# Seven more small loads of x on ScalarE's queue, at the head of a one-token attention and feed-forward kernel

## The chip, the cores and the metric

The kernel runs on one core of one Trainium2 chip. The metric is the device time of one execution in microseconds (us). The kernel before takes 407.94 us, the median of three runs (407.80 to 408.14).

## What is computed

One decode step for one token: an attention block with a key and value cache, then a gated feed-forward block, each behind a layer norm and each added to its input. All tensors are bf16; D = 1024, 32 query heads share 4 key/value heads, the cache holds 65536 positions of 128 numbers, and the feed-forward width is 3584.

```python
h  = x + A(layernorm(x))         # q = x @ wq; softmax(q k^T / sqrt(128)) v; @ wo
h2 = h + B(layernorm(h))         # (gelu(x @ w_gate) * (x @ w_up)) @ w_down
```

Keys and values are 4 x 65536 x 128 numbers each, 67.1 MB apiece; the five weight matrices add 38.8 MB. Nearly all of it is read once and used for one row of x.

## The kernel before

**Staging.** A large SBUF buffer, `ring`, has three slots of 128 partitions x 64 KB. The function `load` (L179 issues the DMA) takes the slots in turn and issues every large load on SyncE's queue, in this order: `wq` (8.39 MB, one slot); then for each key/value head K in two loads and V in two loads of 8.39 MB each, K running one head ahead of V; then `wo`, `w_gate`, `w_up`, and `w_down` in five pieces. A load into a slot waits until the engines have read what the slot held. The texts call the first two K loads K1 and K2 (head 0, first and second half), the third K3 (head 1, first half).

**The head of the kernel.** VectorE clears `x_row` (L183). ScalarE's queue then loads x, 4 rows of 512 bytes, into `x_row` (L184); this is the only load on that queue. The `wq` load is issued by SyncE first of all: a step at the end of the build moves it in front of the start barrier. After L184, ScalarE runs a short exponential (L197, `warm`) that brings in its table. When x has landed, VectorE turns it (`x_t`, L231), the layer norm follows (VectorE, with two short TensorE sums and a power on GpSimd), and its result goes into `xnz` (L238). TensorE then multiplies by `wq` (`q_ps`), once `wq` has landed. The result goes through VectorE (`q_t`, L261) and TensorE into ScalarE's copies into `wsel` (L269).

**The attention loops.** For each half head the K slot is turned in place by VectorE (L288), TensorE forms the scores (`qk_ps`), ScalarE and VectorE make the softmax, and TensorE multiplies by V (`acc_ps`). Near the end of the attention VectorE copies a 32 x 128 block into `o_sb`, a small buffer that nothing touches until then.

**The tail.** The last two loads are halves of the last row block of `w_down`. Four short matmuls (`fb_ps`), one copy (`o_fin`, L601) and the store of the output (L602) follow.

**Completion counters.** Every load on SyncE's and ScalarE's queues counts its completion on one of eight semaphores, DMAHW0 to DMAHW7, which the build hands out in turn over both queues together. A load's counter reaches its mark when all of the load has landed. A load that gets a counter which an earlier load has used waits, on the engine that issues it, until that earlier load has landed. In the kernel before, the first loads have these counters: `wq` 0, x 1, K1 2, K2 3, K3 4; K1 and K2 have no wait at all.

Of the kernel before, what the change touches and what calls it, by code (L numbers as in the profile page):

```python
# [17 lines left out]
def kernel(  # L18
# [13 lines left out]
    nc = tc.nc  # L32
# [50 lines left out]
    o_sb = lead.tile([Hq, Dh], BF16, name="o_sb")  # L83
# [88 lines left out]
    def load(src, off=0):  # L172
        n, w = src.shape[1], src.shape[2]
        if off == 0:
            slot[0] = (slot[0] + 1) % NSLOT
        assert off + n * w <= 2 * CW
        o = slot[0] * 2 * CW + off
        tv = ring[:, o:o + n * w].rearrange("p (n w) -> p n w", w=w)
        loads.append(nc.sync.dma_start(out=tv, in_=src).ins)  # L179
        return tv  # L180
# [3 lines left out]
    nc.scalar.dma_start(out=x_row[0:97:32, :], in_=A_x[0, 0].rearrange("(g n) -> g n", g=4))  # L184
    assert DC * HD == 2 * CW
    wq_t = load(wq_v[:])

    make_identity(nc, ident_bf[:])
    make_identity(nc, ident_f[:])
# [11 lines left out]
    for bp in range(4):  # L201
        s0 = 64 * (bp // 2) + bp % 2
        nc.vector.tensor_copy(out=esel[:, bp, :, :],
                              in_=ident_bf[:, s0:s0 + 63:2].unsqueeze(1).to_broadcast([P, 4, 32]))
# [391 lines left out]
    for b, put in ((0, nc.vector.tensor_copy), (1, nc.scalar.copy)):  # L596
        wv = load(wd_v[:, c0:FC, b * HW:(b + 1) * HW], c0 * D + b * HW)
        down_rows(wv, c0, 1, [b])
        if b == 1:
# [3 lines left out]
                      in_=o_b[0:97:32, :, :])  # L603
# [30 lines left out]
```

## Time and profile before

| | |
|---|---|
| median of three runs | 407.94 us |
| span of the profiled execution, first to last instruction | 406.0 us |
| own time of the profiled execution | not listed apart from its span |
| median of the runs less that span | 1.94 us |
| TensorE busy | 295.5 us (73%) |
| VectorE busy | 203.8 us (50%) |
| ScalarE busy | 40.0 us (10%) |
| SyncE's DMA queue (q1) | 173.02 MB, 98.7% of the time of 16 DMA engines |
| ScalarE's DMA queue (q10) | 8 packets, 2 KB |

The span runs from the first to the last instruction of one profiled execution; the time of a run holds that and what lies around it. Busy shares are averages over the whole span. The share of a DMA queue is the time that its packets took, over the span of all 16 DMA engines. In the timeline, an engine name with a q (SPq, ACTq) is the engine's instruction that issues a DMA, not the transfer.

### The profile page before, as it was taken

The numbers are of one execution on the slowest core, as the hardware profiler recorded it, in microseconds if no ns is written. First come the engines' busy times: TensorE is split into PE (matmuls) and PEld (weight loads), VectorE is DVE, ScalarE is ACT, GpSimd is POOL, SyncE is SP. The second block draws the span as 40 slices with busy tenths as digits, with TensorE's granted clock in tenths as the row PEclk, the third lists the DMA queues.
The fourth block names the chain that finished last, engine by engine and source line by source line (L and its number), as shares of the span: only waits on it lengthen the run. The fifth ranks groups of instructions, "written<-read, shape, count | busy, mean of one in ns | idle before, by whom it ended". The sixth has DMA issues, their size and how long they took to land.

```text
span 406.0 us, 2610 instructions
## 1 busy us (share of the span) xinstructions
PE 295.5 (73%) x1519; PEld 59.4 (15%) x681; DVE 203.8 (50%) x186; ACT 40.0 (10%) x62; POOL 7.5 (2%) x17
## 2 busy tenths in 40 slices
PE   0160777758899695979969957997696999646196
PEld 0110111111111110221111113111110211211012
DVE  0210989999839744971595387609943000220210
ACT  1000000023000031100000302000021100100000
POOL 2000000000000000000000000000010000000000
PEclk9995689987899999769999967899999699886689
DMA  9999999999999999999999999999999999999995
GB/s 413 413 413 471 458 413 415 413 466 452 413 421 420 471 439 413 428 420 471 433 420 428 420 465 433 420 435 420 458 433 420 441 420 458 399 442 447 400 423 225
DMA packets 3631, 173.18 MB, mean 427 GB/s; under 512 B 416, under 2 KB 676, under 8 KB 804
## 3 DMA queue, kind: packets, MB, share of 16 engines
q1 hardware_dynamic: 3612, 173.02, 98.7%
q8 instruction: 8, 0.13, 0.1%
q14 instruction: 3, 0.02, 0.0%
q10 hardware_dynamic: 8, 0.00, 0.0%
HBM read 173.02 MB, written 0.00 MB: 426 GB/s over the span
## 4 chain that ended last, share of the span: by engine, by line
DMA 41%; PE 35%; DVE 21%; ACT 2%; issue 1%; ACTq 0%; DVEq 0%
DMA ring<-in_A_k_cache_dram 30%; DVE ring L288 16%; PE acc_ps L158 16%; DMA ring<-in_B_w_down_dram 11%; PE qk_ps L156 6%; PE qk_ps L158 5%; PE acc_ps L156 5%; DVE mx L313 2%; ACT sc L309 2%; DVE pT L346 1%; PE o_ps L156 1%; PE at_ps L156 1%; DVE acc_sb L369 1%; PE at_ps L158 1%; PE nb_ps L156 0%
## 5 line engine op out<-in xcount | busy, mean ns | idle before, releaser
L288 DVE STREAM_TRANSPOSE ring<-ring 128x2048 uint32<-128x2048 uint32 x64 | 142.6, 2279 | 36.9 <-DMA ring<-in_A_k_cache_dram 36.9
L156 PE MATMUL qk_ps<-ring,wsel 128*128 128x512 bf16 x256 | 107.4, 420 | 50.2 <-DVE ring L288 31.2
L158 PE MATMUL qk_ps<-ring,wsel 128*128 128x512 bf16 x256 | 106.6, 416 | 0.0
L158 PE MATMUL acc_ps<-ring,pT 128*128 128x512 bf16 x384 | 105.1, 383 | 0.0
L156 PEld LDWEIGHTS <-wsel 128*128 128x128 bf16 x256 | 27.1, 106 | 157.3 <-issue 140.4
L156 PE MATMUL acc_ps<-ring,pT 128*128 128x512 bf16 x128 | 49.1, 384 | 0.0
L313 DVE TENSOR_REDUCE mx<-qk_ps 128x1 f32<-128x1024 f32 x16 | 19.5, 1220 | 24.7 <-ACT sc L309 18.7
L346 DVE STREAM_TRANSPOSE pT<-pT 128x1024 bf16<-128x1024 bf16 x16 | 19.3, 1228 | 23.8 <-ACT pT L340 23.8
L309 ACT COPY sc<-qk_ps 128x1024 f32<-128x1024 f32 x12 | 12.1, 1012 | 149.5 <-PE qk_ps L158 149.5
L156 PEld LDWEIGHTS <-pT 128*128 128x128 bf16 x128 | 12.8, 100 | 90.7 <-issue 90.6
L369 DVE COPY acc_sb<-acc_ps 32x512 f32<-32x512 f32 x8 | 5.3, 667 | 29.4 <-PE acc_ps L158 29.3
L340 ACT ACTIVATE pT<-sc,nbias 128x1024 bf16<-128x1024 f32 x12 | 13.7, 1141 | 44.9 <-DVE nbias L332 41.9
L156 PE MATMUL wu_ps<-ring,hnz 128*32 128x448 bf16 x32 | 5.9, 729 | 9.0 <-DMA ring<-in_B_w_up_dram 9.0
L156 PE MATMUL ln_tot<-ln_s,ones_f 128*128 128x1 f32 x8 | 1.9, 312 | 13.5 <-DVE ln_s L210 11.7
L156 PE MATMUL q_ps<-ring,xnz 128*32 128x512 bf16 x32 | 5.0, 598 | 8.9 <-DMA ring<-in_A_wq_dram 8.9
L156 PE MATMUL wg_ps<-ring,hnz 128*32 128x448 bf16 x32 | 5.9, 718 | 7.2 <-DMA ring<-in_B_w_gate_dram 7.2
L156 PE MATMUL o_ps<-sel,acc_sb 128*128 128x8 f32 x32 | 6.6, 335 | 5.8 <-DVE rl L383 5.4
L371 ACT COPY acc_sb<-acc_ps 32x512 f32<-32x512 f32 x8 | 4.6, 578 | 58.6 <-DVE acc_sb L369 58.5
L512 DVE STREAM_TRANSPOSE wu_t<-wu_ps 128x448 f32<-128x448 f32 x2 | 1.2, 630 | 14.2 <-PE wu_ps L156 14.2
L261 DVE STREAM_TRANSPOSE q_t<-q_ps 128x512 f32<-128x512 f32 x2 | 1.3, 694 | 13.8 <-PE q_ps L158 13.8
L512 DVE STREAM_TRANSPOSE wg_t<-wg_ps 128x448 f32<-128x448 f32 x2 | 1.2, 628 | 13.4 <-PE wg_ps L156 13.4
L340 ACT ACTIVATE pT<-qk_ps,nbias 128x1024 bf16<-128x1024 f32 x4 | 4.5, 1114 | 29.8 <-PE acc_ps L158 16.8
(108 smaller groups left out, 94.2 us busy)
## 6 DMA issues: line engine op xcount, KB each, us to landing
ring<-in_B_w_gate_dram SPq DMA_DIRECT2D x1, 7168.0 KB, 35.5
ring<-in_B_w_up_dram SPq DMA_DIRECT2D x1, 7168.0 KB, 38.6
ring<-in_B_w_down_dram SPq DMA_DIRECT2D x1, 4096.0 KB, 39.6
ring<-in_B_w_down_dram SPq DMA_DIRECT2D x1, 2048.0 KB, 43.6
ring<-in_B_w_down_dram SPq DMA_DIRECT2D x1, 768.0 KB, 45.0
ring<-in_B_w_down_dram SPq DMA_DIRECT2D x2, 128.0 KB, 44.8
ring<-in_A_k_cache_dram SPq DMA_DIRECT2D x8, 38.6
ring<-in_A_v_cache_dram SPq DMA_DIRECT2D x8, 34.4
```

What stands on the lines that cost most here:

```text
L156: return pe(t.matmul(out, lhsT=lhsT, rhs=rhs, start=start, stop=stop, tile_position=tile_position, skip_group_check=skip_group_check))
L158: op = t.add_instruction(mybir.InstMatmult(name=nc.get_next_instruction_name(), engine=t.engine, start_tensor_calc=start, stop_tensor_calc ...
L261: nc.vector.transpose(out=q_t[:, k, :], in_=q_banks[k])
L288: dv(nc.vector.transpose(out=kt[:, c * w:(c + 1) * w], in_=kt[:, c * w:(c + 1) * w]))
L309: ac(nc.scalar.copy(out=sc[:], in_=flat))
L313: dv(nc.vector.tensor_reduce(out=state[("mx", g)][:, li:li + 1], in_=flat, axis=AX.X, op=ALU.max))
L340: ac(nc.scalar.activation(out=flat, in_=state.pop(("sc", g, li)), func=ACT.Exp, bias=st["nbias"][:, 0:1], scale=scale, accum_out=st["lpart ...
L346: dv(nc.vector.transpose(out=flat, in_=flat))
L369: dv(nc.vector.tensor_copy(out=acc_sb[sl, :], in_=acc[sl, c, :]))
L371: ac(nc.scalar.copy(out=acc_sb[sl, :], in_=acc[sl, c, :]))
L512: nc.vector.transpose(out=t[:, k, :], in_=banks[k][:, 0:HF * 32])
```

## The change

Seven loads are added in the source behind the `wq` load, on ScalarE's queue. Load i (0 to 6) reads the first 16n numbers of x, with n = 2i + 2, into n partitions x 16 numbers (32 bytes) of `o_sb`: 2, 4, 6, 8, 10, 12 and 14 rows, 56 rows and 1792 bytes in all. `o_sb` is written over before it is read, so nothing that is computed changes.

```diff
     nc.scalar.dma_start(out=x_row[0:97:32, :], in_=A_x[0, 0].rearrange("(g n) -> g n", g=4))
     assert DC * HD == 2 * CW
     wq_t = load(wq_v[:])
+    for i in range(7):
+        n = 2 * i + 2
+        nc.scalar.dma_start(out=o_sb[0:n, i * 16:(i + 1) * 16], in_=A_x[0, 0, 0:16 * n].rearrange("(p n) -> p n", n=16))
 
     make_identity(nc, ident_bf[:])
```

## The prediction

> **What bounds the kernel now.** I read the page first, its slices and its DMA queues.
>
> ```profile
> DMA  9999999999999999999999999999999999999995
> GB/s 413 413 413 471 458 413 415 413 466 452 413 421 420 471 439 413 428 420 471 433 420 428 420 465 433 420 435 420 458 433 420 441 420 458 399 442 447 400 423 225
> DMA packets 3631, 173.18 MB, mean 427 GB/s; under 512 B 416, under 2 KB 676, under 8 KB 804
> ...
> q1 hardware_dynamic: 3612, 173.02, 98.7%
> ```
>
> The reader is to see that the DMA engines are busy in every slice but the last; no other engine comes near (TensorE 73%). SyncE's queue q1 fills 98.7% of the span. In the trace's packet records nearly every 64 KB packet takes 2.418 us on its engine, at the start as at the end, which is 16 x 65536 B / 2.418 us = 433.6 GB/s; 173.02 MB at that rate are 399.0 us. So the kernel is one unbroken stream of loads. The rate is that of a busy engine, so time in which the engines stand idle between two loads does not come back.
>
> The chain that ended last confirms the end of it: the last load, then under 1 us of work and the store.
>
> ```profile
> 358.13 44.71 DMA ring<-in_B_w_down_dram
> 402.84 0.04 issue
> 402.88 0.27 PE fb_ps L156 x4
> 403.15 0.02 issue
> 403.17 0.27 ACT o_fin L601
> ```
>
> Further back this chain names VectorE, TensorE and ScalarE, but only because a load's issue waits for its slot. What matters is whether the issue comes before the load ahead of it has landed. The closest case in SyncE's timeline is the V load issued at 111.83 us; the load ahead of it lands at 119.90 us (packet landings in the trace), so 8.1 us early. The stream never starves there, nor would it if loads and work behind them moved together.
>
> Third, the timeline of the first 30 us, where the change sits.
>
> ```profile
> 0.00 0.38 SPq L179 DMA_DIRECT2D ring<-in_A_wq_dram  x1
> ...
> 0.78 0.81 SPq L179 DMA_DIRECT2D ring<-in_A_k_cache_dram  x2
> ...
> 1.07 1.09 ACTq L184 DMA_DIRECT2D x_row<-in_A_x_dram  x1
> ...
> 3.49 0.20 ACT L197 ACTIVATE warm<-neg_half 128x1 f32<-128x1 f32 x1
> 9.82 0.63 DVE L231 STREAM_TRANSPOSE x_t<-x_row 128x256 bf16<-128x256 bf16 x1 [8.63 <-DMA x_row<-in_A_x_dram]
> ...
> 14.62 0.10 PEld L156 LDWEIGHTS <-xnz 128*32 128x32 bf16 x1 [1.72 <-DVE xnz L238]
> 21.85 0.62 PE L156 MATMUL q_ps<-ring,xnz 128*32 128x512 bf16 x4 [8.87 <-DMA ring<-in_A_wq_dram]
> ```
>
> Two things are to be seen. K1 and K2 are issued at 0.78 us, 21 us before `wq` has landed, so each engine goes from its last `wq` packet straight into K1. And x is wanted late: its layer norm is done at 14.62 us, TensorE waits for `wq` until 21.85 us, so x has 21.85 - 14.62 = 7.2 us to spare.
>
> **What the change moves.** The built order of the two programs, with their waits, shows it. Before:
>
> ```
> SP   ring<-in_A_k_cache_dram 128x32768 x2
> SP   ring<-in_A_k_cache_dram 128x32768 [waits DMAHW0,PE]
> ACT  x_row<-in_A_x_dram 4x256 [waits DVE]
> ```
>
> After:
>
> ```
> SP   ring<-in_A_k_cache_dram 128x32768 [waits DMAHW1]
> SP   ring<-in_A_k_cache_dram 128x32768 [waits DMAHW2]
> SP   ring<-in_A_k_cache_dram 128x32768 [waits DMAHW3,PE]
> ACT  o_sb 2x16 / x_row 4x256 [waits DVE] / o_sb 4x16, 6x16, 8x16, 10x16, 12x16 / o_sb 14x16 [waits DMAHW0]
> ```
>
> The seven loads use up the eight counters. In the built order the load of 2 rows has counter 0, `wq` 1, x 2, the loads of 4 to 12 rows 3 to 7; the load of 14 rows is back at 0, K1 at 1, K2 at 2. So K1 now waits for all of `wq` to land, K2 for x, K3 for the load of 4 rows, and ScalarE's last small load for the first. That wait of K1 is the change.
>
> **The sum: the gap in front of K1.** In the packet records each engine's last `wq` packet ends between 20.99 and 21.48 us, on average 21.26. The last landing is counted at 21.81, and TensorE, which waits for the same landing, starts at 21.85. Take 21.85 us for K1's issue. How long a load takes from issue into an empty stream the trace shows once on this queue, for `wq` itself: issued at 0.00, first packets start between 1.00 and 1.75 us, and they take 2.48 to 3.48 us where later ones take 2.418; they end between 4.08 and 4.58, on average 4.35. Less one plain packet that is an effective start at 4.35 - 2.42 = 1.93 us after issue. K1 then runs effectively from 21.85 + 1.93 = 23.78 us instead of 21.26: 2.52 us lost on each engine. Bounds: if the longer first packets belong to the cold start alone, packets start on average 1.22 us behind the issue and the loss is 21.85 + 1.22 - 21.26 = 1.8 us. The store of the output, the other issue into an empty queue, has its first packet 1.28 us after its issue (403.46 to 404.74) where `wq` has 1.00, but its issue is 0.3 us longer too. At the other end, with those 0.3 us for K1 too, it is 2.8 us. I take 2.5, by `wq`'s row, which is the same queue and the same shape.
>
> **What costs nothing.** K2's wait: x has landed long before. K3 was issued at 28.41 us, when TensorE was done with `q_ps`; the small loads have been served by then, at the latest in the gap, where ScalarE's queue has the engines to itself. ScalarE's issues: seven times at most 1.09 us (x's row) are 7.6 us, plus the wait of the last for the first until about 10 us; behind them stand only the table load and `warm`, and ScalarE's next work (L269) is at 30.35 us. If that cover were gone it would still reach only `wsel`, wanted at 43.53 us. The packets: 56 rows and 56 count writes at x's rates (27 and 9 ns) are 2.0 us over 16 engines, 0.25 us on an engine that has a part of all seven; about half of it falls into the gap. I add 0.1 us. `o_sb`'s later overwriting waits for loads that landed 300 us earlier.
>
> x itself gets the load of 2 rows ahead of it. In the packet records x's rows go out at 6.65 us and its count writes at 9.08 us: one small packet per engine and 2.42 us round between q1's packets. Where an engine has both loads, x is two rounds later, 4.84 us, and has 7.2 to spare: 2.4 us remain. Even past that only `q_ps`, the K work and the slots behind them come later, and the stream has 8.1 us or more in hand.
>
> The sum is 2.5 + 0.1 = 2.6 us. Everything behind K1's landing (41.15 us) moves with the stream, up to the store; against the profiled execution the span becomes 406.0 + 2.6 = 408.6 us, and with the 1.94 us by which the median lies over that span, 410.5 us.
>
> **The rivals.** (a) The gap is shorter. Between the end of `wq`'s issue (0.38) and its first packet (1.00) lie 0.62 us; if only these pass behind the wait, on all engines at once and with plain packets, the loss is 21.85 + 0.62 - 21.26 = 1.2 us; with the issue's own 0.38 before them it is 1.6. With the 0.1 for small packets that is 409.2 to 409.6 us. For it: the store's 256-byte packets took 15 to 18 ns each, no long start. Against it: all 16 first `wq` packets are longer than 2.42 us. The Trainium skill, "DMA: Bandwidth & Descriptors" (section Specifications), gives a first-byte latency of about 0.6 us for loads issued by the sync and scalar engines; by that alone the time would be an estimated 409.2 us. The trace has that figure only behind the end of the issue.
>
> (b) The gap opens, and the time stays: 407.9 us. It needs 2.5 us of idle elsewhere to be regained; q1's own 98.7% leave 5.3 us, of which 1.0 lies before the first packet and over 1 behind the last load. Little speaks for it.
>
> (c) Faster. The engines drift apart in the stream: `wq`'s landings lie within 0.49 us, the last load's within 2.1 us (400.71 to 402.84), with a mean of 401.8. A gap sets all engines off together again; if that drift were mended whole, the end would come 1.0 us earlier. It decides from a gap under 0.2 us, as 1.0 must beat the gap by 0.8; the time would then be about 407.1 us. Against it: the drift at 21 us is small and grows afterwards.
>
> (d) The small packets cost far more than x's: 14 of them on the two engines that have a part of every small load, at 0.1 us each instead of 0.02, are 1.4 us, some of it ahead of `wq`'s last packet. Price: 411.3 to 412 us. For it: 32-byte rows are not in the trace. Against it: 4-byte writes take 9 ns there and 256-byte rows 15 to 18 ns. Of like size is the case that a small load lands so late that K3 or the next V load waits. The skill's same page (section on the increment by 16) says that such a load uses the lowest-numbered engines, one for each row here; by that the first two engines carry a packet of all seven. No run here shows it yet.
>
> **How the numbers follow.** The gap as worked out, 409.7 to 411.2 us: 0.80. (a) 0.08, (b) 0.04, (c) 0.02, (d) 0.06. A measurement of this kernel tells apart about 0.2%, 0.8 us, so (b) is the same, (c) faster, and all others are slower: 0.94. The range goes from 409.3, into (a), to 411.5, into (d).
>
> **What would show it.** In the profile after, the timeline has K1's issue at 21.8 to 22.0 us right behind `wq`'s landing instead of 0.78, with K2's behind it; the packets have none of q1's between about 21.5 and 22.8 us; the stretch of 20 to 25 us shows a DMA share near 0.6; VectorE's first L288 starts at 43.5 to 44 us instead of 41.15; q1's share falls to about 98.1%. ScalarE shows eight issues, L231 starts by 15 us and `q_ps` still at 21.9. The prediction is wrong if K1's issue comes early, if the gap is there and the end does not move, or if a second gap opens behind it.

## The result, and the profile after

| | before | after |
|---|---|---|
| median | 407.87 us (4 runs) | 410.53 us (4 runs) |
| ratio | | 1.0064 (95% interval 1.0052 to 1.0076) |
| span of the profiled execution | 406.0 us | 408.8 us (its own time: 410.55 us) |

The changed kernel is slower by 2.66 us; 410.5 us were forecast, with a range of 409.3 to 411.5.

The page of the changed kernel, slices and DMA queues:

```profile
DMA  9979999999999999999999999999999999999995
...
DMA packets 3743, 173.18 MB, mean 424 GB/s; under 512 B 528, under 2 KB 788, under 8 KB 916
...
q1 hardware_dynamic: 3612, 173.02, 98.2%
...
q10 hardware_dynamic: 120, 0.00, 0.0%
```

One digit has changed: the third slice (20.4 to 30.7 us) stands at 7. SyncE's queue q1 moved the same 3612 packets and 173.02 MB, in 98.2% of a longer span. ScalarE's queue q10 has 120 packets in place of 8, too little to show as a share.

The timeline of the head shows which wait stands there:

```profile
0.00 0.39 SPq L179 DMA_DIRECT2D ring<-in_A_wq_dram  x1
...
1.39 0.59 ACTq L184 DMA_DIRECT2D x_row<-in_A_x_dram  x1
...
2.02 7.85 ACTq L189 DMA_DIRECT2D o_sb<-in_A_x_dram  x6
9.90 1.28 ACT L200 ACT_TABLE_LOAD   x1 [9.90 <-DMA o_sb<-in_A_x_dram]
...
14.49 0.63 DVE L234 STREAM_TRANSPOSE x_t<-x_row 128x256 bf16<-128x256 bf16 x1 [13.28 <-DMA x_row<-in_A_x_dram]
...
21.95 5.50 SPq L179 DMA_DIRECT2D ring<-in_A_k_cache_dram  x3
21.98 0.62 PE L156 MATMUL q_ps<-ring,xnz 128*32 128x512 bf16 x4 [4.32 <-DMA ring<-in_A_wq_dram]
...
43.73 4.50 DVE L291 STREAM_TRANSPOSE ring<-ring 128x2048 uint32<-128x2048 uint32 x2 [15.06 <-DMA ring<-in_A_k_cache_dram]
```

SyncE issues K1 at 21.95 us in place of 0.78. TensorE's first `q_ps` matmul, which waits for the same landing of `wq`, starts 0.03 us behind that issue. VectorE's first work on K1 comes at 43.73 us, 2.58 later than before. SyncE's own waits name the releaser:

```profile
SPq L179 <- DMA ring<-in_A_wq_dram: 21.2, 1, 21.2
```

In the kernel before, a line of nearly the same figures (20.2 us, once) belonged to K3 and cost nothing, because K1 and K2 were queued already. The label alone does not tell whether a wait costs; what the DMA engines still have queued at that time does.

The stretch of the gap, by windows (the columns behind the two times: length, busy time of PE, PEld, DVE, ACT and POOL, then TensorE's clock, the DMA share and GB/s):

```profile
20.00:25.00 5.00, 3.02 (x32) 0.72 (x19) 0.00 (x0) 0.00 (x0) 0.00 (x0) 1.00 0.62 210
```

The kernel before has a share of 0.97 and 419 GB/s there, two packets an engine where this one has one; a packet counts here whole, in the stretch in which it starts. The end of the chain is as it was, later by 2.78 us:

```profile
362.94 42.68 DMA ring<-in_B_w_down_dram
405.62 0.04 issue
405.66 0.26 PE fb_ps L156 x4
405.93 0.02 issue
405.95 0.27 ACT o_fin L604
```

### The profile page after: what moved, and what is told of

Read it like the earlier page. It is cut to its first block, busy times and chain, and to the rows that moved or that the text cites. A ratio compares the mean times of both kernels' runs of the same rounds, so it can differ in the third digit from the quotient of the medians.

```text
span 408.8 us, 2621 instructions
## 1 busy us (share of the span) xinstructions
PE 296.7 (73%) x1519; PEld 58.8 (14%) x681; DVE 203.9 (50%) x186; ACT 40.0 (10%) x62; POOL 7.5 (2%) x17
## 3 DMA queue, kind: packets, MB, share of 16 engines
q1 hardware_dynamic: 3612, 173.02, 98.2%
HBM read 173.02 MB, written 0.00 MB: 423 GB/s over the span
## 4 chain that ended last, share of the span: by engine, by line
DMA 41%; PE 39%; DVE 17%; ACT 2%; issue 1%; ACTq 0%; DVEq 0%
DMA ring<-in_A_k_cache_dram 25%; PE acc_ps L158 16%; DVE ring L291 12%; DMA ring<-in_B_w_down_dram 10%; PE qk_ps L156 8%; PE qk_ps L158 7%; DMA ring<-in_A_wq_dram 5%; PE acc_ps L156 5%; DVE mx L316 2%; ACT sc L312 1%; DVE pT L349 1%; PE o_ps L156 1%; PE at_ps L156 1%; DVE acc_sb L372 1%; PE at_ps L158 1%; ACT acc_sb L374 1%
## 5 line engine op out<-in xcount | busy, mean ns | idle before, releaser
L156 PE MATMUL qk_ps<-ring,wsel 128*128 128x512 bf16 x256 | 108.4, 423 | 53.2 <-DVE ring L291 33.8
L158 PE MATMUL qk_ps<-ring,wsel 128*128 128x512 bf16 x256 | 107.8, 421 | 0.0
```

The costliest lines, as they stand in the source:

```text
L156: return pe(t.matmul(out, lhsT=lhsT, rhs=rhs, start=start, stop=stop, tile_position=tile_position, skip_group_check=skip_group_check))
L158: op = t.add_instruction(mybir.InstMatmult(name=nc.get_next_instruction_name(), engine=t.engine, start_tensor_calc=start, stop_tensor_calc ...
```

## The experiments

The theory: K1 gets the counter that `wq` holds, so it waits until `wq` has landed, and the DMA engines stand idle from `wq`'s last packet until K1's packets flow. The rivals: the small packets on the DMA engines cost the time; ScalarE's issues or the late x do; or part of the gap is regained. Each kernel was timed beside the kernel before, which stood at 407.70 us in the first group (the first four rows) and at 407.87 us in the second; the ratios are to these.

| kernel | K1 issued, us | median, us | ratio (95% interval) |
|---|---|---|---|
| six small loads | 9.49 | 407.78 | 1.0002 (0.9994 to 1.0011) |
| eight small loads | 14.27 | 407.93 | 1.0006 (0.9997 to 1.0014) |
| no small load, K1 waits for `wq` | 22.12 | 410.30 | 1.0062 (1.0050 to 1.0075) |
| no small load, K1 waits for `q_ps` | 27.20 | 416.00 | 1.0202 (1.0188 to 1.0216) |
| two breaks | 21.81; K2 43.69 | 412.92 | 1.0123 (1.0109 to 1.0137) |
| seven small loads, counters handed out otherwise | 9.64 | 407.77 | 1.0000 (0.9991 to 1.0009) |
| fifteen small loads | 23.51 | 412.15 | 1.0105 (1.0091 to 1.0118) |
| the changed kernel again | 21.93 | 410.25 | 1.0059 (1.0046 to 1.0072) |

**Six and eight small loads.**

```diff
-    for i in range(7):
+    for i in range(6):        # the other kernel: range(8)
```

> Six small loads in place of seven (the one of 14 rows is left out). In the built order K1 now has the counter of the load of 2 rows and K2 that of wq. If the wait of K1 for wq is the whole cost, K1 is issued when the load of 2 rows has landed, at about 10 us, long before wq's last packet at 21.3 us; K2 is issued at 21.95 us, with K1 still running until 41 us; no gap opens, and the time is that of the kernel before plus at most 0.1 us: 407.8 to 408.1 us. If the small packets on the DMA engines are the cost, 42 of 56 rows should leave about three quarters of the 2.66 us: about 409.9 us. If ScalarE's issues or the late x are the cost, x lands as late as with seven (14.4 us), and six of seven parts remain: about 410.1 us.

> Eight small loads in place of seven (one of 16 rows is added, 72 rows in all). K1 has x's counter, K2 that of the load of 4 rows; the eighth small load has wq's counter, and it is ScalarE that waits for wq. If the wait of K1 for wq is the whole cost, K1 is issued when x has landed, at about 14.5 us, no gap opens, and more small loads are faster than seven: 407.8 to 408.2 us. ScalarE then issues its last small load at about 22 us and brings its table in by 24.5 us, ahead of its copies into wsel at about 29 us, so that costs nothing. If the small packets or ScalarE's issues are the cost, 72 rows against 56 give about 411.3 us, slower than with seven.

SyncE's issues in the timeline of the first and of the second:

```profile
9.49 19.07 SPq L179 DMA_DIRECT2D ring<-in_A_k_cache_dram  x3
```

```profile
14.27 13.05 SPq L179 DMA_DIRECT2D ring<-in_A_k_cache_dram  x3
...
22.26 1.28 ACT L200 ACT_TABLE_LOAD   x1 [22.26 <-DMA ring<-in_A_wq_dram]
```

With six loads K1 waits for a small load, with eight for x; both issue it well before 21 us, and no gap opens: the DMA share of 20 to 25 us is 0.98 and 0.97. The time is that of the kernel before. With eight the wait for `wq` has moved to ScalarE, whose table load comes at 22.26 us and still ends ahead of its copies into `wsel` at 28.94. Six and eight loads cost nothing and seven cost 2.66 us: a cost that grows with the packets or with the issues cannot give that. x lands as late as with seven (`x_t` at 14.46 and 14.35 us), so the late x is out as well.

**The wait without the small loads.**

```diff
     t = load((k_v if what == "k" else v_v)[g][:, li * LN:(li + n) * LN, :])
+    if len(loads) in (2, 3):
+        tc.add_manual_dep(loads[-1], loads[0].name, ...)      # K1, K2 behind wq
```

> The kernel before, without any small load, but K1 and K2 wait for wq to land. If the wait is the whole cost, the gap is that of the kernel after without the small packets: K1 is issued at 21.85 us, its first packets start 0.95 to 2 us later and are longer than 2.42 us, K1 lands 2.5 us later than in the kernel before, and the time is 410.3 to 410.6 us. If the small loads matter beside the wait, the time lies between 407.9 and 410.2 us, by as much as they cost. x lands at 9.8 us as in the kernel before.

```profile
22.12 6.75 SPq L179 DMA_DIRECT2D ring<-in_A_k_cache_dram  x3
22.14 0.62 PE L156 MATMUL q_ps<-ring,xnz 128*32 128x512 bf16 x4 [9.16 <-DMA ring<-in_A_wq_dram]
```

The wait alone gives 1.0062, the changed kernel gave 1.0064, and the windows show 0.63 as the DMA share of 20 to 25 us, where the changed kernel has 0.62. The whole loss is reproduced without one small load. K1 is issued 0.27 us later than expected, with `wq`'s landing, which this run shows at 22.1 us.

**A gap three times as long.**

```diff
+    q_last = latest["pe"]                # TensorE's last q_ps matmul
...
+    if len(loads) in (2, 3):
+        tc.add_manual_dep(loads[-1], q_last.name, ...)
```

> As the kernel in which K1 waits for wq, but K1 and K2 wait for TensorE's last q_ps matmul, at 27.1 to 28.4 us, so that the gap is three times as long. If the stream regains nothing, the engines lose from 21.26 us to 1.93 us behind K1's issue, 7.8 to 9.1 us, and the time is 415.7 to 417.0 us: each microsecond of later issue is one microsecond of time. If some of a gap is hidden by work elsewhere or given back by a faster stream, the loss is smaller than that, and the gap of 2.5 us was perhaps not lost whole either.

```profile
27.20 1.28 SPq L179 DMA_DIRECT2D ring<-in_A_k_cache_dram  x3
```

K1 is issued 5.08 us later than with the wait for `wq`, and the time rises by 5.7 us, from 410.30 to 416.00; the fastest of its five runs, 415.31, is 5.0 us above. Nothing of a longer gap is regained. From the packet records, the engines lost 7.8 us up to K1's first packets (31.43 us, their mean end, less 2.42 for a plain packet, less 21.21, the mean end of `wq`); the median rose by 8.3. The profiled run of this kernel has a stretch of slightly longer packets between 65 and 155 us, 0.06 to 0.18 us each; behind 30 us its packets take 0.62 us an engine more in all than those of the kernel before. That is about the rest.

**Two breaks.**

```diff
+    if len(loads) in (2, 3):
+        tc.add_manual_dep(loads[-1], loads[-2].name, ...)     # K1 behind wq, K2 behind K1
+    if len(loads) == 4: ...                                   # K3 stays behind K2, without a wait
```

> Without small loads; K1 waits for wq to land and K2 waits for K1 to land, so the stream breaks twice. If each break costs what the first one did, from the last packet of one load to 1.9 us behind the next one's issue, the time is 407.7 + 2 x 2.6 = 412.9 us (412.5 to 413.3). If the long start belongs to the first restart alone, the second break costs 1.8 us: 412.1 us. If the stream regains some of it: below 412 us.

SyncE's timeline from the start, and from 40 us on:

```profile
21.81 22.68 SPq L179 DMA_DIRECT2D ring<-in_A_k_cache_dram  x3
```

```profile
43.69 0.80 SPq L179 DMA_DIRECT2D ring<-in_A_k_cache_dram  x2
```

The windows of the two stretches:

```profile
20.00:25.00 5.00, 3.17 (x32) 0.83 (x19) 0.00 (x0) 0.00 (x0) 0.00 (x0) 1.00 0.61 210
40.00:45.00 5.00, 0.00 (x0) 0.00 (x0) 1.30 (x1) 0.00 (x0) 0.00 (x0) 0.50 1.04 393
```

The first window is as in the changed kernel. The second one's share of 1.04 hides its break, because K2's long first packets, which start from 44.65 us on, count in it whole. The packet records are plain: K1's last packets end at 42.95 us on average, K2's first start between 44.65 and 45.67 and take 3.09 us on average. By the same reckoning as above the first break costs 2.33 us and the second 2.60, together 4.9; the median is 5.05 us over the kernel before. The long first packets come back at the second restart too, so they do not belong to the cold start alone.

**The same seven loads, with other counters.**

```diff
-        nc.scalar.dma_start(out=o_sb[0:n, ...], in_=...)
+        small_x = nc.scalar.dma_start(out=o_sb[0:n, ...], in_=...)
+        tc.add_manual_dep(small_x.ins, loads[0].name, <order only, no wait>)
```

> All seven small loads, with the same sizes, the same queue and the same order on every engine. Only the hand-out of counters differs, by an order edge from wq to each small load: wq now has counter 0 and the load of 2 rows counter 1. So K1 waits for the load of 2 rows, which lands at about 9.5 us, and it is ScalarE's last small load that waits for wq, at 21.9 us. If the collision of counters is the cause, no gap opens and the time is 407.7 to 408.0 us. If the seven loads cost anything by their packets or their issues, that remains: up to 410.4 us.

```profile
0.80 0.55 ACTq L189 DMA_DIRECT2D o_sb<-in_A_x_dram  x1
...
9.64 17.75 SPq L179 DMA_DIRECT2D ring<-in_A_k_cache_dram  x3
...
22.32 1.28 ACT L203 ACT_TABLE_LOAD   x1 [22.32 <-DMA ring<-in_A_wq_dram]
```

The packets, sizes, queue and order of issue on every engine are those of the changed kernel; 120 packets on q10 again. Only `wq` and the load of 2 rows have exchanged their counters. So the last small load now waits for `wq` and is issued at 21.97 us in place of 9.55, and with it ScalarE's table load comes later. The ratio is 1.0000, and the 2.66 us are gone. This is also the mended form of the change: it does not beat the kernel before, which no run did.

**Fifteen small loads.**

```diff
-    for i in range(7):
+    for i in range(15):       # 8 numbers to a row in place of 16
```

> Fifteen small loads in place of seven, of 2 to 30 rows of 16 bytes. Counter 1 now goes from wq to a small load (16 rows) and then to K1: ScalarE waits for wq before it issues that small load, and K1 waits until it has landed. By the collision of counters K1 is issued some 1.5 to 2 us later than with seven loads, at 23.4 to 24.0 us, and the loss is 4.1 to 4.7 us: 411.8 to 412.4 us. If only the number of packets counts, twice the loads cost twice as much: 413 us. With one wait for wq alone, and nothing from the chain behind it: 410.3 us as with seven.

```profile
SPq L179 <- DMA o_sb<-in_A_x_dram: 22.8, 1, 22.8
```

```profile
23.51 3.77 SPq L179 DMA_DIRECT2D ring<-in_A_k_cache_dram  x3
```

SyncE now waits for a small load, which in turn waited for `wq` on ScalarE: that load is issued at 21.82 us, K1 at 23.51. The engines lose 4.1 us up to K1's first packets, and the median is 4.28 us over the kernel before, inside what was expected. The 240 small rows, more than four times those of the changed kernel, account for at most the 0.2 us between the two.

**The changed kernel again.**

> The changed kernel again, beside the others on the same chip: 410.3 to 410.6 us, with K1 issued at 21.9 to 22.1 us. If a stretch of slower packets as in the first profile belongs to the change, it is there again between 100 and 121 us; if it does not, it is elsewhere or absent, and the time is that of the kernel in which K1 waits without small loads, 410.3 us, plus at most 0.1.

```profile
21.93 5.71 SPq L179 DMA_DIRECT2D ring<-in_A_k_cache_dram  x3
```

410.25 us, 2.38 us over its kernel before and 0.05 under what was expected. The slower stretch of the first profile, between 101 and 122 us, is absent.

## Why the prediction was right

**The cause** was the step "K1 now waits for all of `wq` to land". It was read from the built order and its waits, and shown by undoing the collision with all seven loads in place (1.0000) and by making the wait without them (1.0062).

**The size of the gap** was put at 2.52 us, from the issue of `wq` at 0.00. In the first profile after, `wq`'s last packets end at 21.28 us on average and K1's first at 26.20; less a plain packet of 2.42 that is 2.50 us. Two parts of it were each off by 0.1 and cancelled, which is luck: K1 was issued at 21.95 us, not at 21.85, because `wq`'s last landing was counted at 21.94, not at 21.81; and the effective start came 1.83 us behind K1's issue (26.20 - 2.42 - 21.95), not 1.93. As forecast, the first packets were long, 2.42 to 3.37 us, on average 3.06. From the mean end of `wq` the gap is made up of 0.33 us until the last engine has ended (21.61), 0.33 until its landing is counted (21.94), 0.34 until K1's issue is over (22.28), 0.63 until the first packet (22.91), 0.24 more until the mean start (23.15) and 0.64 by which the first packets are longer than a plain one.

**The 0.1 us for small packets** is not seen: the kernels with six, seven and eight loads and no gap stand at 1.0002, 1.0000 and 1.0006, and the wait without small loads costs as much as with them. The term is below what these runs can tell, and the sum came out right with or without it. Rows of 32 bytes took 9 ns each, like the count writes, so rival (d) had no ground.

**Span and time.** Forecast were 408.6 us of span and 1.94 us around it; measured 408.8 and 1.75. Both are off by 0.2 and cancel, so that the median was met within 0.03 us is luck; the second median, 410.25 us, is 0.25 off the forecast. The 0.2 us more in the span lie behind K1: its landing moved by 2.58 us, the last load's by 2.78. The packet records of that run show 55 packets of 64 KB between 101 and 122 us that took 0.06 to 0.14 us longer; in the second profile of the same kernel that stretch is absent and the span is 408.4 us. So it does not belong to the change.

**What costs nothing** held. ScalarE's eight issues took 0.31 to 0.59 us each, and its table load came at 9.90 us. x came two rounds later, `x_t` at 14.49 in place of 9.82 us: 4.67 where 4.84 was put. TensorE had its weights at 19.29 us and still waited 2.7 us for `wq`. Of x's four rows two left at 6.60 and 6.67 us, as before, and two at 11.54 and 11.62, two rounds of 2.42 us behind the load of 2 rows; as forecast, a small packet goes out once in such a round.

**The rivals.** (a), the shorter gap, needed plain first packets; they were long in every run with a break, 3.06 to 3.17 us on average. The trace bears out its 0.62 us only from the end of the issue: K1's issue ends at 22.28 us, and its first packet starts at 22.91, 0.63 later. The Trainium skill, "DMA: Bandwidth & Descriptors" (section Specifications), states a first-byte latency of about 0.6 us; that agrees, from the end of the issue on, and is less than half of what a broken stream loses here. (b), the gap regained, falls with the gap three times as long and with the two breaks. (c), engines set off together, is not seen: the landings of the last load still lie 1.84 us apart (403.78 to 405.62), and in the kernel with eight small loads, without a gap, 1.73 (401.02 to 402.75).

## What to carry to other kernels

In a kernel whose DMA stream never stops, a new wait on the queue that feeds it costs what it drains the stream by, here about 2.5 us for each break in which a load waits for the landing of the load ahead, however small the loads that caused it. Completion counters handed out in turn make a load depend on whatever had its counter eight loads ago, on any queue; so a load added anywhere can hang a big load on another big one, and six or eight of them can be free where seven are not. Read the waits of the built order, not only the diff, and see to it that a long load's counter is next used by something that can wait.

## What the runs showed of the hardware that was not expected

- In the runs with a break the first 64 KB packets behind it took 2.42 to 3.63 us, those that started last being among the shortest; on average 3.06 and 3.09 us in the kernel with two breaks, against 2.42 in the stream.
- A small load, issued when `wq` had landed and no large load was queued, took 1.69 us from its issue to the issue of the load that waited for it (21.82 to 23.51 us, the kernel with fifteen).
- With fifteen loads, q10 shows 160 count writes for 240 small rows and 4 of x. The Trainium skill, "DMA: Bandwidth & Descriptors" (section Why a DMA increments its semaphore by 16 and not by 1), says that a load runs on the largest number of engines up to 16 that divides its rows, each with one count: 2 + 4 + ... + 16 for the first eight loads, 9 + 10 + ... + 15 for those of 18 to 30 rows, and 4 for x, which is 72 + 84 + 4 = 160. The trace agrees.
